# An earlier weight split and two later loads in a LayerNorm, attention and feed-forward kernel

## The chip, the cores and the metric

The kernel runs on one core of a Trainium2 chip. The metric is the device time of one execution in microseconds (us); lower is better. The core has five engines that each work through their own instructions in order: TensorE (PE: matrix products), VectorE (DVE), ScalarE (ACT), GpSimd (POOL) and SyncE (SP, which here only issues transfers). They wait for each other by semaphores. Transfers between memory and the on-chip buffers run on 16 DMA engines.

## The reference

```python
x  = A_x                                   # 2048 x 576
xn = layernorm(x)                          # (x - mean) / sqrt(var + 1e-5)
# A: local dilated attention, 32 heads of 18
q, k, v = split(xn @ wqkv)                 # wqkv: 576 x 1728
idx = pos[:, None] - 2 * arange(8)         # 8 positions, two apart; negative ones masked
attn = softmax(where(mask, q . k[idx] * 18 ** -0.5, -1e9))
A = (attn . v[idx]) @ wo
# B: feed-forward, 576 -> 4608 -> 576
h = relu(xn @ w1 + b1); h = h * h
B = h @ w2 + b2
out = x + A + B
```

Everything is float32.

## The kernel before

**Tiling.** The 2048 positions are four blocks (`b` = 0 to 3) of 512. The Q, K, V weights are four groups (`g` = 0 to 3, eight heads each). A "row" is one call of `qkv_row(b, g, j, i)`: 14 matmuls (L304) that give K, V and Q of 128 positions for one group; ScalarE copies the product out (L296) and issues its store to the scratch tensors `kvq` (L298), from which the attention later loads its rows.

**Split operands.** To keep float32 precision, each matmul operand is held as a high half (rounded by ScalarE) and a low half (the rest, subtracted by VectorE, L95). For the Q, K, V weights this is `split_wq(g, name)`: three high halves (`wq_hi`, L262) and three low halves (`wq_lo`, tiles `h`, `S` or `w1s` from the raw tiles `r`), handed out in three steps. Its last step may call a function, here the load of another group, because the raw tiles share four buffers: a new group can come only as low halves free them. A row of group g needs `split_wq(g)` to be done.

**Normalization.** Means and inverse deviations of block 1 are turned by TensorE, written to memory and read back spread over all partitions as tile `mb` (`load_mb`, L172). `normalize(b)` then subtracts and multiplies in place (tiles `w1r`, `w2r`), and makes the halves `X` and `x`: 8 steps. A row of block b needs it to be done.

**Order of the work.** The engines' order is the order of the program. Side work is written as generators: `run(pieces, k)` takes k steps from the list `pieces`, and when that is empty, from the attention queue (`side`). The attention of a block and group runs on VectorE in such steps; `offer(b, g)` queues it and its loads (`fetch`: tiles `q` and `kv`, on SP at first, later on GpSimd).

- `q0` does rows 0 to 25 before the first feed-forward pair: rows 0 to 3 are group 1 of block 0, 4 to 7 group 3, 8 to 11 group 2, and from row 12 on they are block 1. At r = 2 it issues `load_wq(2)` and `load_mb(1)`.
- `phase_a` runs the feed-forward of two blocks in 18 pairs of hidden tiles (`ffn_pair`, L524, L528, L493), `phase_b0` the second product of block 1 (tiles n = 0 to 35, 14 matmuls each, L493) together with the normalization and the rows of blocks 2 and 3. `load_w2(i)` brings the w2 tiles through three buffers, `load_h` the stored hidden tiles. `load_xt(3)` brings x of block 3 (L157, L160) into a buffer that block 0's output (`finish`, L757, L758) has to leave first.

Of the kernel before, what the change touches and what calls it, by code (L numbers as in the profile page):

```python
# [45 lines left out]
def block_kernel(ctx: ExitStack, tc: tile.TileContext, x, xt, wqkv, wo, w1, b1, w2, b2, out):  # L46
# [47 lines left out]
    def tt(out, a, b, op):  # L94
        return nc.vector.tensor_tensor(out=out, in0=a, in1=b, op=op)  # L95
# [14 lines left out]
    def open_x(b):  # L110
        X[b] = mt.tile([P, 2, NC - 1, TB], F32R, name=f"X{b % 2}")
        x4[b] = mt.tile([P, TB], F32R, name=f"x4{b % 2}")

    def four(dt=F32):
        return sb.tile([P, 2, TB], dt, name="r4", bufs=4)
# [39 lines left out]
    def load_xt(b):  # L155
        xm[b] = sb.tile([P, NC - 1, TB], F32, name="w1r", bufs=2)
        nc.sync.dma_start(xm[b], xt[b, :, :NC - 1])  # L157
        xf[b] = {1: lambda: sb.tile([P, DE], F32, name="w2r", bufs=3)[:, :TB],
                 2: lambda: sb.tile([P, TB], F32, name="xf"), 3: lambda: four()[:, 0]}[b]()
        nc.sync.dma_start(xf[b], xt[b, :, NC - 1])  # L160
# [13 lines left out]
    def normalize(b):  # L174
        open_x(b)
        for a in (0, 2):
            v = xm[b][:, a:a + 2]
            for k, op in enumerate((ALU.subtract, ALU.mult)):
                tt(v, v, mb[b][:, k:k + 1].to_broadcast([P, 2, TB]), op)
                if k:  # L180
                    nc.scalar.activation(X[b][:, 0, a:a + 2], v, AF.Copy)
                yield
        for k, op in enumerate((ALU.subtract, ALU.mult)):
            tt(xf[b], xf[b], mb[b][:, k], op)
        left_hi(x4[b], xf[b])
        yield
        for a in (0, 2):
            tt(X[b][:, 1, a:a + 2], xm[b][:, a:a + 2], X[b][:, 0, a:a + 2].bitcast(F32), ALU.subtract)
            yield
        left_lo(x4[b], xf[b])  # L190
        normed.add(b)
        yield

    def left_hi(to, v):
        nc.scalar.activation(to, v, AF.Copy)

    def left_lo(to, v):
        tt(to[64:], v[64:], to[64:].bitcast(F32), ALU.subtract)
# [49 lines left out]
    def load_wq(g, ks=range(3)):  # L248
        for k in ks:
            n = 2 if k < 2 else 1  # L250
            r = raws[g, k] = sb.tile([P, 2, QW], F32, name="r4", bufs=4)[:, :n]
            nc.sync.dma_start(r, wqkv[g, :, 2 * k:2 * k + n])
# [14 lines left out]
    def split_wq(g, name, then=lambda: None):  # L267
        open_wq(g, name)
        for k in range(4):
            if k < 3:  # L270
                wq_hi(g, k)
            if k:
                wq_lo(g, k - 1)
                if k == 3:
                    then()
                    split_up.add(g)
                yield
# [132 lines left out]
    def run(gens, k):  # L410

        while k > 0 and gens:
            try:
                next(gens[0])
                k -= 1
            except StopIteration:
                gens.pop(0)
        side(k)
# [355 lines left out]
    def phase_b0():  # L774
        b, r = 1, 0
        todo = [(2 + i, g, j) for g in range(G) for i in range(2) for j in range(NJ)]
        split_up.clear()
        open_stage()
        load_xt(3)
        load_wq(0)  # L780
        pieces = [normalize(2), once(load_mb, 3), split_wq(0, "S", lambda: load_wq(1)), normalize(3)]
        open_y(b)
        for n in range(NF):
            w2_hi()
            if n % 2 == 0:
                h_hi(0, n // 2 + 1)
            add(b, tile_products(b, n, hs[0, n // 2]))
            w2_lo()
            if n % 2 == 0:
                h_lo(0, n // 2 + 1)  # L790
            if n % 2 and n // 2 + 3 < NP:
                load_h(0, n // 2 + 3)
            run(pieces, 1 + n % 2 if n < 9 else 1)
            while r < 32 and 32 * (n - 6) > 22 * r:
                bb, g, j = todo[r]
                while bb not in normed or g not in split_up:
                    run(pieces, 1)
                qkv_row(bb, g, j, 2 + r % 3)
                r += 1
                if r == 2:  # L800
                    pieces.append(split_wq(1, "w1s", lambda: load_wq(2)))
                if r == 8:
                    pieces.append(split_wq(2, "S", lambda: load_wq(3)))
                if r == 16:
                    pieces.append(split_wq(3, "w1s"))
                if r == 24:
                    pieces.append(sums(1))
                if j == NJ - 1 and bb == 2:
                    offer(2, g)
                run(pieces, 2)  # L810
            if n == 20:
                load_w1(NP)
            if n == 25:
                assert not any(a != "x" and c < 2 for a, c, _ in loads)
                held[0] = True
            if n == 28:
                run_all(pieces)
                last_sum(1)
                complete(1)
                regroup(b, 0)  # L820
                regroup(b, 1)
                held[0] = False
                fetch()
                load_w1(NP + 1)
                for g in range(G):
                    offer(3, g)
            if n == 31:
                combine_w1(NP)
            if n == 33:
                residual(b)  # L830
            if n in (32, 33):
                c = 2 * (n - 32)
                o_hi(b, c), o_hi(b, c + 1)
                o_lo(b, c), o_lo(b, c + 1)
        o_hi(b, 4)
        o_lo(b, 4)
        open_left(b)
        load_left(b)
        for c in range(3):
            w2_hi()  # L840
            add(b, o_ops(b, c))
            w2_lo()
            if c == 1:
                w1_hi(NP, 0)
                w1_lo(NP, 0)

        def filler(i):
            if i < 2:
                add(b, o_ops(b, 3 + i), range(NC) if i else ())
            if i == 0:  # L850
                w1_hi(NP, 1)
                w1_lo(NP, 1)
            if i == 1:
                finish(b)

        return filler
# [247 lines left out]
    def q0():  # L1104
        todo = [(b, g, j) for b, g in ((0, 1), (0, 3), (0, 2), (1, 3), (1, 2), (1, 1), (1, 0)) for j in range(NJ)]
        pieces = [statistics(1), split_wq(3, "S")]

        waiting = []

        def row(r):  # L1110
            b, g, j = todo[r]
            while b and b not in normed or g not in split_up:
                run(pieces, 1)
            qkv_row(b, g, j, r % 5)
            if j == NJ - 1:
                def go(b=b, g=g):
                    offer(b, g)
                    if not b and g > 1:
                        offer({3: 2, 2: 3}[g])

                if r < 6:
                    waiting.append(go)
                else:
                    go()

        for r in range(len(todo) - 2):
            row(r)
            if r == 2:
                turn_mr(1, 7)
                run_all(pieces)  # L1130
                load_wq(2)
                load_mb(1)
                pieces += [normalize(1)]
            if r == 6:
                offer(0, 0)
                for late in waiting:
                    late()
                waiting.clear()
                lane[0] = nc.gpsimd
                pieces.insert(0, split_wq(2, "h", lambda: load_wq(0)))  # L1140
            if r == 10:
                load_w1(0)
            if r == 11:
                run_all(pieces)
            if r == 15:
                pieces.append(sums(0))
            if r == 19:
                split_up.discard(0)
                pieces.insert(0, split_wq(0, "h"))
            if r == 21:  # L1150
                run_all(pieces)
                for n in range(3):
                    load_w2(n)
                combine_w1(0)
                load_w1(1)
            if r in (24, 25):
                w1_hi(0, r - 24)
                w1_lo(0, r - 24)
            elif r != 3:
                run(pieces, 3 if r < 1 or 15 <= r < 20 else 1 if r > 20 else 2)  # L1160

        def filler(i):
            if i < 2:
                row(len(todo) - 2 + i)
            if i == 1:
                last_sum(0)

        return filler
# [68 lines left out]
```

## Time and profile before

| | |
|---|---|
| median of 3 runs | 1132.63 us (1131.63 to 1132.97) |
| profiled execution, its time | 1132.16 us |
| its span, first to last instruction | 1130.5 us |
| mean granted TensorE clock | 0.997 of full speed |
| DMA traffic | 216.50 MB, mean 192 GB/s |

A profile shows one execution. Timeline lines read: start and duration in us, engine, line of the kernel, operation, tiles out<-in, count, and in brackets how long the engine had stood idle and what ended that. "A <- B: total, times, longest" is a line of the list of waits. SPq lines are transfers being issued by SP, not their landing; a landing time counts from issue to the end of the transfer. Times are from the start of the span.

### The profile page before, as it was taken

How to read it: one execution, taken by the hardware profiler on the slowest of the kernel's cores; microseconds unless marked ns; L12 is line 12 of the kernel's file. 1: busy time of each engine (PE TensorE's matmuls, PEld its weight loads, DVE VectorE, ACT ScalarE, POOL GpSimd, SP SyncE). 2: the span in 40 equal slices, each digit the busy share in tenths (PEclk: the TensorE clock that was granted, in tenths of full speed). 3: DMA queues.
4: the chain of work that ended last, by engine and by line, in shares of the span. 5: the costliest groups of instructions: out<-in, count | busy, mean ns of one | idle time of the engine just before them, and what ended most of it. 6: DMA issues, size and time to landing. Idle time of an engine off the chain costs nothing.

```text
span 1130.5 us, 13846 instructions
## 1 busy us (share of the span) xinstructions
PE 1114.8 (99%) x5014; PEld 938.1 (83%) x5014; DVE 915.0 (81%) x1202; ACT 575.7 (51%) x801; POOL 118.1 (10%) x219
## 2 busy tenths in 40 slices
PE   9799999999999999999999999999999999999998
PEld 7699888888888888788889888888888888888887
DVE  7596888887978887779888979898989888786463
ACT  5334756566565654543333446656656566533341
POOL 4001001030200210001020101010202020101000
PEclk9899999999999999999999999999999999999999
DMA  8855546375583658865674855454545362568552
GB/s 291 294 197 168 162 140 205 121 151 202 170 218 101 214 195 284 285 222 182 226 270 131 316 167 174 161 180 137 191 146 197 129 210 95 179 210 300 180 170 89
DMA packets 88965, 216.50 MB, mean 192 GB/s; under 512 B 11960, under 2 KB 40384, under 8 KB 83520
## 3 DMA queue, kind: packets, MB, share of 16 engines
q1 hardware_dynamic: 52464, 148.95, 38.8%
q0 software_dynamic: 10544, 52.14, 14.5%
q10 hardware_dynamic: 25888, 14.53, 4.2%
q8 instruction: 39, 0.64, 0.2%
q14 instruction: 30, 0.25, 0.1%
HBM read 173.03 MB, written 42.55 MB: 191 GB/s over the span
## 4 chain that ended last, share of the span: by engine, by line
PE 90%; DVE 3%; DMA 2%; ACT 2%; issue 1%; POOL 0%; ACTq 0%; DVEq 0%; POOLq 0%; SPq 0%
PE p L493 42%; PE p L524 29%; PE p L304 13%; PE p L528 5%; DMA w2r<-in_w 1%; DVE w1s L95 1%; DMA mb<-mr 1%; PE p L1021 1%; DVE w2s L95 1%; DVE w1r L95 0%; ACT st L296 0%; POOL kvq L1173 0%; ACT h L535 0%; ACTq L298 0%; ACT w2s L466 0%
## 5 line engine op out<-in xcount | busy, mean ns | idle before, releaser
L493 PE MATMUL p<-h,w2s 128*128 128x512 f32 x2010 | 484.7, 390 | 2.2 <-ACT h L767 0.9
L493 PEld LDWEIGHTS p<-h,w2s 128*128 128x128 f32 x2010 | 376.8, 188 | 83.1 <-ACT h L767 1.3
L524 PE MATMUL p<-X,w1s 128*128 128x512 f32 x864 | 219.5, 389 | 0.2 <-DVE w1s L95 0.2
L524 PEld LDWEIGHTS p<-X,w1s 128*128 128x128 f32 x864 | 162.1, 188 | 34.1 <-DVE w1s L95 0.6
L95 DVE TENSOR_TENSOR w2s<-w2r,w2s 128x576 fp32r<-128x576 f32 x164 | 123.4, 754 | 65.5 <-ACT w2s L466 63.7
L466 ACT ACTIVATE w2s<-w2r 128x640 fp32r<-128x640 f32 x164 | 120.1, 734 | 109.9 <-PE p L493 91.3
L524 PE MATMUL p<-S,w1s 128*128 128x512 f32 x648 | 164.6, 389 | 0.0
L524 PEld LDWEIGHTS p<-S,w1s 128*128 128x128 f32 x648 | 121.5, 188 | 25.5 <-DVE r L95 0.3
L381 POOL DMA_DIRECT2D o<-q x128 | 69.4, 607 | 597.5 <-DVE q L95 595.7
L95 DVE TENSOR_TENSOR w1s<-w1r,w1s 128x1024 fp32r<-128x1024 f32 x72 | 88.1, 1224 | 33.6 <-ACT w1s L439 33.5
L531 ACT ACTIVATE r<-r,b1t 128x512 f32<-128x512 f32 x72 | 51.9, 721 | 107.6 <-DVE r L95 107.5
L296 ACT ACTIVATE st<-p 128x432 f32<-128x432 f32 x64 | 33.8, 529 | 117.0 <-PE p L304 107.4
L95 DVE TENSOR_TENSOR pr<-q,kv 128x1152 f32<-128x1152 f32 x64 | 86.8, 1356 | 1.6
L95 DVE TENSOR_TENSOR pr<-lg,kv 128x1152 f32<-128x1152 f32 x64 | 86.6, 1353 | 0.8
L353 DVE TENSOR_REDUCE lg<-pr 128x64 f32<-128x1152 f32 x64 | 86.4, 1349 | 0.8
L95 DVE TENSOR_TENSOR pr<-pr 128x576 f32<-128x576 f32 (+1 forms) x128 | 77.7, 607 | 3.8
L439 ACT ACTIVATE w1s<-w1r 128x1024 fp32r<-128x1024 f32 x72 | 75.7, 1052 | 5.1 <-PE p L493 4.2
L539 ACT ACTIVATE r<-r 128x1024 f32<-128x1024 f32 x72 | 75.4, 1051 | 0.1
L95 DVE TENSOR_TENSOR h<-r,h 128x1024 fp32r<-128x1024 f32 (+2 forms) x42 | 49.2, 1180 | 27.6 <-ACT r L539 23.8
L528 PE MATMUL p<-x,w1s 128*128 128x512 f32 x216 | 66.5, 389 | 0.0
L95 DVE TENSOR_TENSOR r<-p,r 128x512 f32<-128x512 f32 (+1 forms) x76 | 52.2, 687 | 13.0 <-ACT r L589 10.1
L304 PE MATMUL p<-w1s,X 128*128 128x432 f32 x288 | 60.3, 358 | 0.0
(138 smaller groups left out, 1115.5 us busy)
## 6 DMA issues: line engine op xcount, KB each, us to landing
w2r<-in_w SPq DMA_DIRECT2D x144, 320.0 KB, 3.1
kv<-kvq POOLq DMA_DIRECT2D x29, 1296.0 KB, 6.9
w1r<-in_w SPq DMA_DIRECT2D x36, 640.0 KB, 4.4
h<-r SPq DMA_DIRECT2D x36, 512.0 KB, 3.0
h<-h SPq DMA_DIRECT2D x36, 512.0 KB, 4.1
kvq<-st ACTq DMA_DIRECT2D x64, 216.0 KB, 2.9
r<-in_wqkv SPq DMA_DIRECT2D x16, 432.0 KB, 5.8
w2r<-in_wo SPq DMA_DIRECT2D x20, 320.0 KB, 3.0
```

Source lines behind the costliest of these rows:

```text
L95: return nc.vector.tensor_tensor(out=out, in0=a, in1=b, op=op)
L296: nc.scalar.activation(stage[0][:, j], p[:, :QW], AF.Copy)
L304: nc.tensor.matmul(p[:, :QW], l, r, start=k == 0, stop=k == len(mm) - 1)
L353: nc.vector.tensor_reduce(out=lg[:, j * HG:(j + 1) * HG].rearrange("p a w -> p w a"), in_=pr.rearrange("p w (a d) -> p w a d", d=DH), axis ...
L381: nc.gpsimd.dma_start(rows[:, i], q[i * L:(i + 1) * L, :, a:z])
L439: nc.scalar.activation(w1s[n, k][:, 0], raw1[n][:, 4 * k:4 * k + 4], AF.Copy)
L466: nc.scalar.activation(w2s[stream[i]][:, :DE], raw2[i], AF.Copy)
L493: nc.tensor.matmul(yp[b][c], v, a, start=c not in yb[b], stop=c in last and c not in [o[0] for o in ops[i + 1:]], skip_group_check=True)
L524: nc.tensor.matmul(to, l, r, start=start and i == 0, stop=i == len(mm) - 1, skip_group_check=True)
L528: nc.tensor.matmul(to, weight(LEFT, k, f), v, start=False, stop=k == 1, skip_group_check=True)
L531: nc.scalar.activation(to, a, AF.Relu, bias=b1t[:, f:f + 1])
L539: nc.scalar.activation(r, r, AF.Square)
```

## The change

Two edits. In `q0` the split of group 2 (whose last step calls `load_wq(0)`) is put into `pieces` at r = 4, in front of `normalize(1)`; before, `normalize(1)` was put there at r = 2 and the split was put ahead of what was left of it at r = 6. Since `load_wq(0)` is called from the split, its three transfers now stand ahead of the first attention loads (`offer(0, 0)` and the waiting offer, at r = 6) in SP's queue. In `phase_b0` the call `load_xt(3)` moves from the start to behind tile n = 3.

```diff
@@ phase_b0
         open_stage()
-        load_xt(3)
         load_wq(0)
         pieces = [normalize(2), once(load_mb, 3), split_wq(0, "S", lambda: load_wq(1)), normalize(3)]
...
                 run(pieces, 2)
+            if n == 3:
+                load_xt(3)
             if n == 20:
                 load_w1(NP)
@@ q0
                 run_all(pieces)
                 load_wq(2)
                 load_mb(1)
-                pieces += [normalize(1)]
+            if r == 4:
+                pieces += [split_wq(2, "h", lambda: load_wq(0)), normalize(1)]
             if r == 6:
                 offer(0, 0)
                 for late in waiting:
                     late()
                 waiting.clear()
                 lane[0] = nc.gpsimd
-                pieces.insert(0, split_wq(2, "h", lambda: load_wq(0)))
```

Instruction by instruction, the orders of TensorE and GpSimd stay as they were. On ScalarE and VectorE group 2's split now stands in front of the whole normalization of block 1, and two steps of the first attention come behind the sums of x (`sums(0)`) instead of ahead of them; from there the attention steps stand a little later among the first feed-forward pairs, until the orders agree again. On SP the three transfers of group 0 go ahead of the five first attention loads, and x of block 3 goes behind the h load of tile 3.

## The prediction

> **What bounds the kernel now.** I read the page first, then the list of waits of TensorE, then the timelines of the two places that this list names, engine by engine, then landing times and windows.
>
> ```profile
> span 1130.5 us, 13846 instructions
> ...
> PE 1114.8 (99%) x5014; PEld 938.1 (83%) x5014; DVE 915.0 (81%) x1202; ACT 575.7 (51%) x801; POOL 118.1 (10%) x219
> ...
> PE 90%; DVE 3%; DMA 2%; ACT 2%; issue 1%; POOL 0%; ACTq 0%; DVEq 0%; POOLq 0%; SPq 0%
> ```
> TensorE is busy for 99% of the span and carries 90% of the chain that ended last. So only time in which TensorE stands still, or runs slowly, can be won; other engines count only where TensorE waits for them. Its waits:
> ```profile
> PE p L304 <- ACT h L262: 6.8, 1, 6.8
> ...
> PE p L493 <- ACT h L767: 0.9, 1, 0.9
> PE p L493 <- ACT w2s L466: 0.8, 1, 0.8
> ```
> One wait stands out: a Q, K, V row (L304) for the high half of a weight group (L262). The two small ones (L767, L466) lie in phase_b0. The change touches exactly these two places.
>
> **Place one: group 2's split and block 1's normalization.** TensorE's timeline (start, duration):
> ```profile
> 40.72 2.50 PE L304 MATMUL p<-S,X 128*128 128x432 f32 x12
> ...
> 50.37 4.61 PE L304 MATMUL p<-h,X 128*128 128x432 f32 x12 [6.75 <-ACT h L262]
> ...
> 55.20 2.52 PE L304 MATMUL p<-h,X 128*128 128x432 f32 x12
> ```
> These are rows r = 7, 8 and 9 (each has 2 more matmuls behind these 12). A row takes 2.75 us at full speed: the chain has two rows in 5.49, in a line shown further down. Row 8, the first that reads group 2, could start at 40.72 + 2.75 = 43.47 and row 9 at 46.22. Row 9 started at 55.20: **8.98 us lost**, 6.75 idle and the rest a slow row 8 (4.61 for 2.51). The clock tells why; in this row of the windows view PEclk is the field before the last two:
> ```profile
> 50.00:55.00 5.00, 4.63 (x13) 3.82 (x14) 4.59 (x6) 2.00 (x4) 0.00 (x0) 0.57 1.00 369
> ```
> The granted clock was 0.57 right behind the gap, so without the gap the slow row goes too. The Trainium skill ("TensorE: Matmul & The Clock Gate", Part 1) says that an idle window of about 3.4 us halves the clock and a busy one restores it. By it, half speed for 3.4 us would cost 1.7 us, an estimate, and the loss would be 8.45 us, which would put the sum 0.5 us higher. The row measures 4.61 - 2.51 = 2.1 us and more in its end; I keep the 8.98.
>
> Why was group 2 late? VectorE, ScalarE and the load queue:
> ```profile
> 40.31 4.88 DVE L95 TENSOR_TENSOR w1r<-w1r,mb 128x1024 f32<-128x1024 f32 x4 [8.13 <-DMA mb<-mr]
> ...
> 50.35 2.54 DVE L95 TENSOR_TENSOR h<-r,h 128x864 fp32r<-128x864 f32 x3 [2.70 <-ACT h L262]
> 52.81 1.22 DVE L95 TENSOR_TENSOR X<-w1r,X 128x1024 fp32r<-128x1024 f32 x1
> 54.06 0.69 DVE L95 TENSOR_TENSOR x<-w2r,x 64x512 fp32r<-64x512 f32 x1
> 54.78 1.36 DVE L95 TENSOR_TENSOR pr<-q,kv 128x1152 f32<-128x1152 f32 x1
> ```
> ```profile
> 49.39 2.19 ACT L262 ACTIVATE h<-r 128x864 fp32r<-128x864 f32 x3 [0.49 <-ACT st L296]
> ```
> ```profile
> 31.55 1.31 SPq L252 DMA_DIRECT2D r<-in_wqkv  x3
> 33.38 0.33 SPq L172 DMA_DIRECT2D mb<-mr  x1
> ...
> 34.27 1.01 SPq L326 DMA_DIRECT2D kv<-kvq  x2
> ...
> 48.96 3.77 SPq L252 DMA_DIRECT2D r<-in_wqkv  x3
> ```
> Landing times, from the transfers of 29 to 45 us and from those of tile kv:
> ```profile
> r<-in_wqkv SPq DMA_DIRECT2D x2, 432.0 KB, 4.1
> ...
> r<-in_wqkv SPq DMA_DIRECT2D x1, 216.0 KB, 4.5
> ```
> ```profile
> DMA to landing us min/median/max: 6.6/9.9/12.3
> ```
> Group 2's raw weights were issued from 31.55 to 32.86, so they had landed by about 37.4. But their split stood behind the normalization, and that waited for mb until 40.31: VectorE stood idle for 8.13 us with the split's work at hand.
>
> **The change there.** No arithmetic is added or removed. I go through the new order.
>
> The split now stands behind row 4's output on ScalarE. Row 4 starts three rows before row 7, at 32.47, and ends at 35.22. From the first high half to the last low half the split took 50.35 + 2.54 - 49.39 = 3.50 us. Begun when row 4 ends, it would be done at 38.7; begun only when the last piece is in, at 40.9. I take 39.9, since the first piece lands near 35.7 (31.55 + 4.1) and row 4's output comes first. Row 8 needs it at 43.47: 3.6 us of cover, 2.6 at the late end. If this cover went, each microsecond beyond it would be TensorE's. **Gain 8.98 us.**
>
> The normalization comes behind it. mb had landed at 40.31; it now shares the queue with fewer bytes, so I take no later time for it. Before, VectorE did its part ahead of the split from 40.31 to 47.65 (50.35 less the 2.70 idle), 7.34 us, and its part behind from 52.81 to 54.75, 1.94 us. So it ends at 49.6 instead of 54.75. Row 12, the first of block 1, starts at 43.47 + 4 x 2.75 = 54.5: 4.9 us of cover.
>
> The queue: load_wq(0)'s three transfers move ahead of the first q and kv loads, and two of them wait for buffers that the split's first two low halves free, the second a little before the split's end. All five attention loads and load_w1(0) queue behind that. Near the split's end q goes, and the first K load near 40.3, 6 us later than before. Bounds for its landing from the tile's row: 46.9 (40.3 + 6.6) and 52.6 (40.3 + 12.3). The slowest before had a second kv load, mb and group 2 before it; I take 48, near the lower middle, because here only 648 KB of late group 0 pieces are ahead of q and K. VectorE wants K at 49.6. So it is free at 48, and 3.0 us late at worst. The Trainium skill ("DMA: Bandwidth & Descriptors", Queues, rings and completion order) speaks against this step: descriptors on an engine are consumed in ring order and a completion lands only behind that engine's earlier writes. By it alone K could not pass those transfers; the late K is a rival below, priced from rows. Nothing in this trace has K behind group 0's transfers.
>
> Does the earlier start survive to the feed-forward part?
> ```profile
> 70.49 1.25 DVE L95 TENSOR_TENSOR pr<-pr 128x576 f32<-128x576 f32 x2
> ...
> 73.40 1.22 DVE L95 TENSOR_TENSOR w1r<-w1r 128x1024 f32<-128x1024 f32 x1
> ...
> 101.34 1.23 DVE L95 TENSOR_TENSOR w1s<-w1r,w1s 128x1024 fp32r<-128x1024 f32 x1 [1.30 <-ACT w1s L439]
> ```
> ```profile
> 101.81 0.61 PE L524 MATMUL p<-X,w1s 128*128 128x512 f32 x2
> ```
> ```profile
> sum 320.00, PE 319.64 PEld 264.97 DVE 266.50 ACT 192.05 POOL 38.62; mean PE 18.80 PEld 15.59 DVE 15.68 ACT 11.30 POOL 2.27
> ```
> In the new order two steps of the first attention come behind the sums: 73.40 - 70.49 = 2.91 us less before them. The sums then start at 49.6 + (73.40 - 54.78) - 2.91 = 65.3, which is 8.1 us earlier. VectorE's work from there to the first w1 low half is the same. It was free at 100.04, 1.30 us before that step; now at 91.9. TensorE needs the step 8.98 us earlier, at 92.36. So 0.4 us are left, and K may land 0.4 us after 49.6. The two steps fall into the feed-forward pairs, where the windows from 100 to 420 us sum to PE 319.64 of 320 and DVE 266.50: VectorE has 53 us to spare. No cost.
>
> **Place two: x of block 3.**
> ```profile
> 443.27 15.25 PE L493 MATMUL p<-h,w2s 128*128 128x512 f32 x66 [0.16 <-DVE w1r L747]
> ...
> 463.63 6.64 PE L493 MATMUL p<-h,w2s 128*128 128x512 f32 x28 [0.89 <-ACT h L767]
> ```
> ```profile
> 450.64 7.75 DMA w2r<-in_w
> ...
> 470.27 5.49 PE p L304 x28
> 475.76 3.19 PE p L493 x14
> ```
> ```profile
> 445.94 0.51 SPq L758 DMA_DIRECT2D out<-r  x1
> 448.06 0.36 SPq L157 DMA_DIRECT2D w1r<-in_xt  x1
> ...
> 448.94 1.66 SPq L252 DMA_DIRECT2D r<-in_wqkv  x3
> 450.64 1.05 SPq L456 DMA_DIRECT2D w2r<-in_w  x2
> ```
> ```profile
> w2r<-in_w SPq DMA_DIRECT2D x144, 320.0 KB, 3.1
> ...
> w1r<-in_xt SPq DMA_DIRECT2D x6, 1024.0 KB, 6.9
> ```
> The queue stood at 446.45 until 448.06, when block 0's output had left x's buffer, then sent x and group 0, and only then w2 for tile 5. That w2 took 7.75 us, to 458.39, with its split still to come; TensorE waited 0.75 for it (the 0.8 of the waits), and the 0.89 behind it follows, since ScalarE and VectorE ran late after it. Without both, tile 5 starts at 458.52 and three tiles of 3.19 end at 468.09, against 470.27: **gain 2.18 us**. In the new order w2 is issued near 448.1 and lands between 451.2 (3.1) and 455.9 (7.75). Even then 2.6 us are left for its split before 458.52.
>
> ```profile
> 472.98 4.88 DVE L95 TENSOR_TENSOR w1r<-w1r,mb 128x1024 f32<-128x1024 f32 x4 [0.56 <-DMA mb<-mr]
> ```
> x now goes out behind the h load of tile 3, when that tile ends near 455.3, and lands near 462.2. Queued behind it: w2 for tiles 9 and 10, the next h load, mb of block 3. Tile 9 begins near 468.1 + 5.5 + 3.2 = 476.8, and x itself is wanted by VectorE's normalization near 472.98 - 2.18 = 470.8. About 14 and 8 us of cover: no cost.
>
> **Sum.** The profiled execution took 1132.16 us; minus 8.98 and 2.18 is 1121.0. The median of the runs is 0.47 higher, so 1121.4. In a measurement of this kernel 0.2% (2.3 us) is about what can be told from no change.
>
> **Rivals.**
> *Place two gives nothing* (w2 is held by something else, or x hurts where it now stands): for it, the earlier w2 waits from 432 on show the queue crowded there; against it, the cover above. 1121.4 + 2.2 = 1123.6. Chance 0.10.
> *The first K load is late*: for it, the row's maximum; against it, the bytes in flight. At 52.6, less the 0.4 us of slack, it costs 2.6 us: 1124.0. Chance 0.09.
> *The split does not come early* (weights land late, or ScalarE is held): for it, landing times vary; against it, 2.6 to 3.6 us of cover. Place one is lost in full only if the split still ends after mb's work: 1130.4. Chance 0.04.
> *Slower*: K gates all of VectorE's in-order work up to the feed-forward start, each microsecond beyond 50.0 costs one. It beats 11.2 us of gain and adds 0.2% only if K lands after 50.0 + 11.2 + 2.3 = 63.5, 23 us after its issue, nearly twice the longest row; then 1135 or more. Chance 0.03.
>
> **The numbers.** The forecast holds 0.74. The range goes from 1120.0 (the runs scatter by 0.7 either way, and some further hidden delay may go at place two) to 1124.3, which takes in the first two rivals. Faster by over 0.2%: 0.95; within: 0.02; slower: 0.03.
>
> **What would show it.** Right: the 6.75 us wait is gone, the granted clock stays at 1.0 from 40 to 60 us, row 9 starts near 46.2, the feed-forward part near 92.8, and the waits on L466 and L767 in phase_b0 are gone. Wrong: VectorE idle before its first attention step with a kv transfer as releaser, a longer wait of TensorE on w1s near 93, or a new wait in phase_b0 behind x's load.

## The result and the profile after

The changed kernel took **1124.77 us** (median of 6 runs, 1123.5 to 1125.66), the kernel before 1132.62 (6 runs, 1131.49 to 1133.38): a ratio of 0.9931, with a 95% interval of 0.9918 to 0.9944. It is faster by 7.9 us; the forecast was 11.2, and 1124.77 lies 0.5 us above the top of its range. The profiled execution took 1125.13 us. From its page:

```profile
span 1123.4 us, 13847 instructions
...
PE 1112.8 (99%) x5014; PEld 938.1 (84%) x5014; DVE 914.7 (81%) x1202; ACT 575.7 (51%) x801; POOL 117.7 (10%) x219
...
PE 87%; DVE 6%; DMA 3%; ACT 2%; issue 1%; SPq 0%; ACTq 0%; POOL 0%; DVEq 0%; POOLq 0%
```
TensorE's share of the chain that ended last fell from 90 to 87%, VectorE's rose from 3 to 6% and DMA's from 2 to 3%: somewhere the chain now runs through other engines instead of through matmuls. The list of TensorE's waits says where:
```profile
PE p L524 <- DVE w1s L95: 2.6, 1, 2.6
...
PE p L493 <- ACT h L767: 0.2, 1, 0.2
```
The 6.8 us on L262 are gone, and so are L466's 0.8 and most of L767's 0.9, as forecast. New is a wait of 2.6 us at the start of the feed-forward part (L524). TensorE's timeline at place one, rows 7, 8 and 9 (each line is the 12 long matmuls of a row), and the windows view there (the field before the last two is the granted clock):
```profile
42.21 2.50 PE L304 MATMUL p<-S,X 128*128 128x432 f32 x12
...
44.94 2.51 PE L304 MATMUL p<-h,X 128*128 128x432 f32 x12
...
47.68 2.52 PE L304 MATMUL p<-h,X 128*128 128x432 f32 x12
```
```profile
50.00:55.00 5.00, 5.00 (x28) 4.80 (x27) 2.79 (x3) 2.54 (x4) 0.00 (x0) 1.00 1.01 421
```
No gap, no slow row, and the clock is 1.00 where it was 0.57. To see where the rest of the time went, four points of TensorE's timeline are compared: the first row (r = 0), the first feed-forward matmul, the second group of these matmuls, and the first row of phase_b0. Before:
```profile
21.42 2.50 PE L304 MATMUL p<-w1s,X 128*128 128x432 f32 x12
...
102.62 1.19 PE L524 MATMUL p<-X,w1s 128*128 128x512 f32 x4 [0.19 <-DVE w1s L95]
...
470.11 2.51 PE L304 MATMUL p<-S,X 128*128 128x432 f32 x12
```
After:
```profile
22.90 2.52 PE L304 MATMUL p<-w1s,X 128*128 128x432 f32 x12
...
94.29 0.61 PE L524 MATMUL p<-X,w1s 128*128 128x512 f32 x2
97.48 1.19 PE L524 MATMUL p<-X,w1s 128*128 128x512 f32 x4 [2.57 <-DVE w1s L95]
98.74 1.53 PE L524 MATMUL p<-S,w1s 128*128 128x512 f32 x6
...
463.07 2.51 PE L304 MATMUL p<-S,X 128*128 128x432 f32 x12
```
(102.62 is the group behind the prediction's row at 101.81.)

| stretch | before, us | after, us | difference | forecast |
|---|---|---|---|---|
| start to r = 0 | 21.42 | 22.90 | +1.48 | 0 |
| r = 0 to the first L524 | 80.39 | 71.39 | **-9.00** | -8.98 |
| first L524 to its second group | 0.81 | 3.19 | **+2.38** | 0 |
| second group to the first row of phase_b0 | 367.49 | 365.59 | -1.90 | -2.18 |
| from there to the end of the span | 660.39 | 660.33 | -0.06 | 0 |

The sum is -7.10, which is the difference of the spans. Of the 4.1 us by which the profiles fall short of the forecast, 2.38 are the new wait, 1.48 a later start of the rows and 0.28 place two.

**Where the new wait begins** is 40 us earlier. VectorE (start, duration, and in brackets its idle time and releaser):
```profile
38.85 2.55 DVE L95 TENSOR_TENSOR h<-r,h 128x864 fp32r<-128x864 f32 x3 [5.18 <-ACT h L262]
41.71 4.88 DVE L95 TENSOR_TENSOR w1r<-w1r,mb 128x1024 f32<-128x1024 f32 x4 [0.32 <-DMA mb<-mr]
...
52.14 1.22 DVE L95 TENSOR_TENSOR X<-w1r,X 128x1024 fp32r<-128x1024 f32 x1 [3.09 <-ACT X L181]
...
54.12 1.36 DVE L95 TENSOR_TENSOR pr<-q,kv 128x1152 f32<-128x1152 f32 x1
```
The split is done at 41.4 and the normalization starts at once, but inside it VectorE stands for 3.09 us, because ScalarE has not made the second high half of X (L181). ScalarE (ACTq is a transfer that it issues):
```profile
44.23 1.06 ACT L181 ACTIVATE X<-w1r 128x1024 fp32r<-128x1024 f32 x1 [1.29 <-DVE w1r L95]
45.20 0.51 ACT L296 ACTIVATE st<-p 128x432 f32<-128x432 f32 x1
50.64 0.37 ACTq L298 DMA_DIRECT2D kvq<-st  x1
51.05 1.06 ACT L181 ACTIVATE X<-w1r 128x1024 fp32r<-128x1024 f32 x1 [5.34 <-DMA kv<-kvq]
```
Between X's two high halves, in program order, stand the output of row 7 (L296) and its store (L298). The output was copied at 45.7; the store went out at 50.64, and the bracket names a kv load as what ended ScalarE's 5.34 us. A store of row 7 uses no data of that load. The chain of waits gives the links with their times:
```profile
34.73 8.44 DMA kvq<-st
...
43.24 7.32 DMA kv<-kvq
...
50.64 0.37 ACTq L298
...
51.05 1.07 ACT X L181
```
In the built program the transfers of SP and ScalarE report their end on eight semaphores in rotation, and a transfer is issued only when the one before it on its semaphore has landed. The store of row 3 (34.73), the first K load (43.24) and the store of row 7 (50.64) have the same one; in the trace's records it is number 100 for all three, and each goes out just after the one before has landed (43.17, then 43.24; 50.56, then 50.64). So K was issued, though it reads other rows, 1.5 us after the queue had reached it (the q load ahead of it went out at 41.32 and took 0.38), when row 3's store landed; row 7's store had to wait for K; and X's second high half stood behind that store in ScalarE's order. Attention began at 54.12. The forecast's 49.6, moved by the 1.48 of the late start, is 51.08: 3.04 us later, and less the forecast's 0.4 us of slack that gives 2.6, against 2.38 measured at the feed-forward start.

### The profile page after: what moved, and what is told of

The parts are those of the page before. It is cut to its first block, busy times and chain, and to the rows that moved or that the text cites. A ratio compares the mean times of both kernels' runs of the same rounds, so it can differ in the third digit from the quotient of the medians.

```text
span 1123.4 us, 13847 instructions
## 1 busy us (share of the span) xinstructions
PE 1112.8 (99%) x5014; PEld 938.1 (84%) x5014; DVE 914.7 (81%) x1202; ACT 575.7 (51%) x801; POOL 117.7 (10%) x219
## 4 chain that ended last, share of the span: by engine, by line
PE 87%; DVE 6%; DMA 3%; ACT 2%; issue 1%; SPq 0%; ACTq 0%; POOL 0%; DVEq 0%; POOLq 0%
PE p L493 42%; PE p L524 29%; PE p L304 9%; PE p L528 5%; DVE pr L95 1%; PE p L1022 1%; DMA kvq<-st 1%; DVE w1s L95 1%; DMA kv<-kvq 1%; DMA w2r<-in_w 1%; DVE r L95 1%; DVE lg L353 0%; DVE w1r L95 0%; DVE w2s L95 0%; DMA r<-in_wqkv 0%
## 5 line engine op out<-in xcount | busy, mean ns | idle before, releaser
L524 PE MATMUL p<-X,w1s 128*128 128x512 f32 x864 | 219.5, 389 | 2.6 <-DVE w1s L95 2.6
L524 PEld LDWEIGHTS p<-X,w1s 128*128 128x128 f32 x864 | 162.1, 188 | 36.5 <-DVE w1s L95 3.0
L466 ACT ACTIVATE w2s<-w2r 128x640 fp32r<-128x640 f32 x164 | 120.1, 734 | 110.6 <-PE p L493 92.9
L524 PE MATMUL p<-S,w1s 128*128 128x512 f32 x648 | 164.6, 389 | 0.0
L524 PEld LDWEIGHTS p<-S,w1s 128*128 128x128 f32 x648 | 121.4, 188 | 25.5 <-DVE r L95 0.2
L296 ACT ACTIVATE st<-p 128x432 f32<-128x432 f32 x64 | 33.8, 528 | 104.5 <-PE p L304 89.7
```

The costliest lines, as they stand in the source:

```text
L296: nc.scalar.activation(stage[0][:, j], p[:, :QW], AF.Copy)
L466: nc.scalar.activation(w2s[stream[i]][:, :DE], raw2[i], AF.Copy)
L524: nc.tensor.matmul(to, l, r, start=start and i == 0, stop=i == len(mm) - 1, skip_group_check=True)
```

## The experiments

The first four ran on one chip, the next three on another, the last two on the first again, each group beside runs of the kernel before (1132.09, 1132.57 and 1132.32 us). In the texts on record theory A is the one above: a store on ScalarE that cannot go out until the K load has landed costs the 2.4 us at the feed-forward start. Its rivals put the missing time at place two (B), at a K load or queue that is late for VectorE itself (C), or into attention steps that were moved and are paid for later (D).

**Edit 1 alone** (before, with the split moved to r = 4 and x of block 3 left where it was).

```diff
     # q0
-                pieces += [normalize(1)]
+            if r == 4:
+                pieces += [split_wq(2, "h", lambda: load_wq(0)), normalize(1)]
...
-                pieces.insert(0, split_wq(2, "h", lambda: load_wq(0)))
```


> Edit one alone (group 2's split first), x of block 3 left where it was. Theory A (a store of ScalarE that waits for the first K load gives part of place one back): place one is worth 8.98 less 2.4, and place two is missing, 1.8 by the two profiles: 1126.6 us, with TensorE's 2.6 us wait on w1s still there. Theory B (place two gave nothing, as the first rival said): 1124.8, as with both edits.

Measured: 1128.3 us (1126.94 to 1131.65), ratio 0.9969, interval 0.9957 to 0.9981. TensorE's timeline at the feed-forward start:
```profile
96.63 1.19 PE L524 MATMUL p<-X,w1s 128*128 128x512 f32 x4 [3.00 <-DVE w1s L95]
```
The new wait is here too, without the second edit: it belongs to the split. By this profile (1127.09 us) the span from r = 0 (21.60) to 96.63 is 75.03 us, where before has 81.20: 6.17 of the 8.98 are left. Behind 96.63 this profile is 0.89 us longer than before, with 1.3 us of waits on L466 instead of 0.8. The median of the runs is only 3.8 below before: 1.7 us above theory A's 1126.6, and further still from B's 1124.8. The four runs with a mean granted clock of 1.000 took 1126.94 to 1128.42, so the clock does not explain it all; the rest stays open.

**Edit 2 alone** (before, with only `load_xt(3)` moved).

```diff
     # phase_b0
-        load_xt(3)
...
+            if n == 3:
+                load_xt(3)
```


> Edit two alone (x of block 3 behind tile 3). Theory A and the profiles: the two waits on L466 and L767 go, 1.8 us less than before: 1130.8 us. The prediction's own term: 2.18 less, 1130.4. The first rival: no change, 1132.6.

Measured: 1130.71 us (1129.25 to 1131.28), ratio 0.9985, interval 0.9976 to 0.9993. TensorE:
```profile
102.35 1.20 PE L524 MATMUL p<-X,w1s 128*128 128x512 f32 x4 [0.17 <-DVE w1s L95]
...
461.23 6.66 PE L493 MATMUL p<-h,w2s 128*128 128x512 f32 x28 [0.16 <-ACT h L767]
467.72 2.51 PE L304 MATMUL p<-S,X 128*128 128x432 f32 x12
```
From 102.35 to 467.72 are 365.37 us, where before took 367.49: 2.12 less, against 2.18 forecast. The rival "place two gives nothing" falls. In runs the gain is 1.4 (0.8 to 2.7 by the interval). The two edits taken singly give 3.8 + 1.4 = 5.2 us, and both together 6.5 to 7.9 in three measurements. Of the difference, 0.9 us by the profiles is what edit 1 alone loses behind the feed-forward start; the rest is open.

**X's high halves ahead of row 7's store** (changed kernel; four steps at r = 6 and none at r = 7, so that ScalarE makes the rest of the high halves before row 7's output; nothing is added or left out).

```diff
-                run(pieces, 3 if r < 1 or 15 <= r < 20 else 1 if r > 20 else 2)
+                run(pieces, 3 if r < 1 or 15 <= r < 20 else 1 if r > 20 else 4 if r == 6 else 0 if r == 7 else 2)
```


> The changed kernel with block 1's normalization steps 4 and 5 in front of row 7, so that ScalarE makes X's second high half and x4's before it comes to the store of row 7; VectorE's and SP's orders and every transfer stay. Theory A (the store, which waits for the first K load, held ScalarE for 5 us and with it X's high half): VectorE's 3.1 us of idle in the normalization goes, the w1s wait falls from 2.6 to about 0.2 us, 2.4 us less: 1122.4 us. Theory C (the first K load or the queue itself is late, so VectorE would wait anyway) and theory D (the two attention steps moved behind the sums cost it): no change, 1124.8.

Measured: 1122.53 us (1121.73 to 1122.6), ratio 0.9915, interval 0.9902 to 0.9927. ScalarE, VectorE and TensorE:
```profile
49.48 0.37 ACTq L298 DMA_DIRECT2D kvq<-st  x1
```
```profile
46.67 2.35 DVE L95 TENSOR_TENSOR X<-w1r,X 128x1024 fp32r<-128x1024 f32 x2
...
49.77 1.36 DVE L95 TENSOR_TENSOR pr<-q,kv 128x1152 f32<-128x1152 f32 x1
...
64.33 0.42 DVE L363 TENSOR_REDUCE sm<-lg 128x32 f32<-128x256 f32 x1 [2.09 <-ACT lg L361]
```
```profile
94.74 1.19 PE L524 MATMUL p<-X,w1s 128*128 128x512 f32 x4 [0.75 <-DVE w1s L95]
```
Row 7's store is as late as before, but nothing that VectorE wants stands behind it. X's two low halves follow each other, attention begins at 49.77, and the wait at the feed-forward start falls from 2.57 to 0.75. This shows the cause: only the order on ScalarE changed; the instructions of the other engines stand in the same order. From r = 0 (21.96) to the second group the profile has 72.78 us, where the changed kernel has 74.58: 1.80 less. The 2.2 us between the medians are not all from this, since this profile's r = 0 also came 0.94 earlier. Theory A had expected a wait of 0.2; what is left comes from 64.33, where VectorE has waited 2.09 us for an attention step on ScalarE behind other late stores (0.56 in the kernel before).

**The attention loads ahead of group 0's** (changed kernel; the queue order of the kernel before, with the split still early).

```diff
-                pieces += [split_wq(2, "h", lambda: load_wq(0)), normalize(1)]
+                pieces += [split_wq(2, "h"), normalize(1)]
...
                 lane[0] = nc.gpsimd
+                load_wq(0)
```


> The changed kernel, but group 0's raw weights are loaded behind the five first attention loads, as before the change; the split stays early. K then lands some 4 to 6 us sooner. Theory C (K's landing sets it): the wait on w1s is gone, 1122.4 us. Theory A: by the built program the stores of rows 5, 6 and 7 then share completion semaphores with the first q load, the third kv load and a weight load, so the store of row 6, ahead of both high halves of X, waits for the third kv load (near 50 us): the normalization is late again, 1124.8 to 1127 us.

Measured: 1131.0 us (1129.74 to 1132.42), ratio 0.9991, interval 0.9982 to 0.9999. ScalarE, then TensorE:
```profile
52.73 0.37 ACTq L298 DMA_DIRECT2D kvq<-st  x1
53.14 1.06 ACT L181 ACTIVATE X<-w1r 128x1024 fp32r<-128x1024 f32 x1 [11.05 <-DMA kv<-kvq]
```
```profile
101.49 2.07 PE L524 MATMUL p<-X,w1s 128*128 128x512 f32 x4 [4.30 <-DVE w1s L95]
```
Of SyncE's queue:
```profile
34.73 1.06 SPq L326 DMA_DIRECT2D kv<-kvq  x2
...
42.37 0.39 SPq L326 DMA_DIRECT2D kv<-kvq  x1
```
The first two kv loads go out at 34.73 instead of 43.24, and it is worse. Fewer bytes ahead of K should have helped if K's landing for VectorE were the trouble; K landed at 44.31, and theory C falls. Theory A has the reason: in the built program the store of row 6 shares a semaphore with the third kv load (42.37, landed at 52.65) and stands in front of both high halves of X; the one at 53.14 is the first. ScalarE stood 11.05 us instead of 5.34. The direction was expected, the price (1124.8 to 1127 us) was underrated: TensorE waited 1.19 and 4.30 us at the feed-forward start, and the granted clock was 0.84 and then 0.50 there (95 to 100 and 100 to 105 us).

**The changed kernel again** (no edit).

> The changed kernel once more, nothing edited, for its start: in its first profile the first row of the Q, K, V part (r = 0) began at 22.90 us, 1.48 later than in the profile before. If that is scatter from run to run, this profile shows r = 0 between 21.4 and 22.9, as the other runs' (21.60 to 21.96), and 1124.8 us in the median; if the change itself delays the start, 22.9 again.

Measured: 1126.11 us (1124.38 to 1128.77), ratio 0.9943, interval 0.9931 to 0.9956. Its profiled execution was the slowest of these runs, 1128.77. TensorE and the windows view:
```profile
98.42 2.07 PE L524 MATMUL p<-X,w1s 128*128 128x512 f32 x4 [3.49 <-DVE w1s L95]
...
100.72 2.76 PE L524 MATMUL p<-S,w1s 128*128 128x512 f32 x6
```
```profile
95.00:100.00 5.00, 1.58 (x4) 1.29 (x5) 4.90 (x7) 1.10 (x2) 0.00 (x0) 0.72 0.16 48
100.00:105.00 5.00, 5.00 (x17) 4.11 (x16) 0.95 (x3) 0.58 (x1) 0.00 (x0) 0.60 0.38 131
```
The same wait was 3.49 us here and the clock fell behind it; the two groups of matmuls took 2.07 and 2.76 us, for 1.19 and 1.53 in the first profile, 2.1 us more. The wait itself is not its whole price: the slower clock behind it comes on top. The start, for which this was run, was late again: r = 0 began at 22.92.

**Two attention steps fewer ahead of the feed-forward** (X's high halves first, and no step at r = 14 either).

```diff
-                ... else 4 if r == 6 else 0 if r == 7 else 2)
+                ... else 4 if r == 6 else 0 if r in (7, 14) else 2)
```


> The kernel with the halves first, and two further attention steps (the end of the softmax and one product, 2.6 us of VectorE) behind the sums: no step at r = 14. Theory A: what is left of the w1s wait there, 0.75 us, comes from VectorE being 2.1 us late behind an exponential that stands on ScalarE behind held-up stores; with 2.6 us less ahead of the feed-forward part the wait goes to about 0.2: 1122.0 us. Theory D (attention steps moved later are paid for in the feed-forward pairs): 1122.5 or more, with waits of TensorE there.

Measured: 1123.86 us (1123.24 to 1126.06), ratio 0.9928, interval 0.9915 to 0.9942. TensorE:
```profile
94.15 1.20 PE L524 MATMUL p<-X,w1s 128*128 128x512 f32 x4 [0.17 <-DVE w1s L95]
...
634.75 3.51 PE L493 MATMUL p<-h,w2s 128*128 128x512 f32 x14 [0.88 <-ACT w2s L466]
...
639.31 9.86 PE L493 MATMUL p<-w1s,w2s 128*128 128x512 f32 x42 [1.05 <-ACT w2s L466]
```
The wait at the start is down to 0.17, but two new ones of 0.88 and 1.05 stand 540 us later in the profile. This fits theory D, by which a step left for later is paid for elsewhere, but does not show it. The attention steps stand in another order all the way to these waits, and ahead of the first of them ScalarE had waited 3.47 us for an h tile (1.53 in the kernel with the high halves first). A wait of this size also comes without an edit: the second profile of that kernel has one of 1.30 us (on L747, at 436.11), the first has not. The version is no better than the one without this step.

**The gap filled** (before, with 26 bf16 matmuls on constant data ahead of row 8; extra work into an unused result).

```diff
+            if r == 7:
+                idle = bank(7)
+                for _ in range(26):
+                    nc.tensor.matmul(idle, warm[:, :P], warm, start=True, stop=True)
```


> The kernel before, with 26 matmuls on constant data (about 5.7 us, results unused) between row 7 and row 8, so that TensorE is busy in the 6.75 us gap; nothing else changes and the gap stays as long. If the slow row 8 (4.61 us for 2.51) is the price of the clock that fell in the gap, row 8 takes 2.5 us up to its own wait for low halves, the granted clock stays at 1.0, and the time falls by 1.0 to 2.1 us: 1130.0 to 1131.1. If row 8 is slow because it waits for the low halves piece by piece, it stays slow: 1132.1.

Measured: 1131.68 us (1131.13 to 1134.18), ratio 0.9996, interval 0.9987 to 1.0004. TensorE and the windows view:
```profile
43.92 5.56 PE L1144 MATMUL p<-lg 128*128 128x512 bf16 x25
50.97 0.67 PE L304 MATMUL p<-h,X 128*128 128x432 f32 x2 [1.49 <-ACT h L262]
52.06 3.78 PE L304 MATMUL p<-h,X 128*128 128x432 f32 x10 [0.43 <-DVE h L95]
```
```profile
50.00:55.00 5.00, 3.60 (x10) 3.03 (x11) 4.02 (x5) 2.60 (x4) 0.00 (x0) 0.72 0.98 344
```
This was to tell how much of the slow row 8 is the clock's. It is inconclusive: the clock fell to 0.72 all the same, after 1.49 us of idle time.

**The changed kernel a third time, and X's high halves first a second time**, side by side (no new edit).

> The changed kernel a third time, side by side with the next one. Theory A: a wait on w1s of 2.5 to 3.5 us, 1124.5 to 1126.5 us. Its first row (r = 0), at 22.9 us in both profiles so far: 21.4 to 22.0 if that was chance, 22.9 if it belongs to this kernel.

> The kernel with the halves first once more, on the same chip as the changed kernel: theory A gives a wait on w1s under 1 us and 2 to 3 us less than the changed kernel, 1122 to 1123 us. If the first result came from another chip or chance, the two agree.

Measured: 1125.35 us (1123.71 to 1127.66), ratio 0.9935 (0.9921 to 0.9948), and 1122.11 us (1121.57 to 1123.67), ratio 0.991 (0.9896 to 0.9924). The second kernel's row:
```profile
94.39 1.20 PE L524 MATMUL p<-X,w1s 128*128 128x512 f32 x4 [0.75 <-DVE w1s L95]
```
Its wait is 0.75 again, where the changed kernel's was 3.37 (with a granted clock of 0.81 from 95 to 100 us). The changed kernel's r = 0 began at 23.20, this one's at 21.62. The version with X's high halves first is the best of all that ran: 3.2 us below the changed kernel here (part of it the start), 2.2 in the first measurement of each, and some 10 below the kernel before.

## Why the prediction was right or wrong

*Place one, the gain of 8.98: right.* From r = 0 to the first feed-forward matmul the time fell by 9.00. Moved by the late start, the split's end at 39.9 becomes 41.38; it was 41.40. Row 9 at 46.22 becomes 47.70; it was 47.68. The prediction's lower figure of 8.45 was 0.5 short. That the slow row 8 would go with the gap was right as well. The filled gap did not settle how much of it was the clock's, but the clock records in the trace of before do: half speed from 47.50 to 54.33 us, which covers the first 3.96 us of the row that began at 50.37 and so accounts for 1.98 of its 2.10 us.

*The queue and the normalization, "so it is free at 48": this step failed.* K landed at 50.56 (43.24 + 7.32), inside the bounds (46.9 to 52.6, moved by 1.48) and half a microsecond before VectorE would have taken it, at 51.03 (54.12 - 3.09). So the transfer that was asked about was in time. But the step counted VectorE's own time alone (7.34 and 1.94 us) and knew one waiter for K, VectorE's first attention step. The other was row 7's store on ScalarE, and with it everything queued behind that store, X's second high half first. The normalization therefore ended 3.04 us later than forecast, and that went through to the feed-forward start, as the step "K may land 0.4 us after 49.6" had said of any lateness there: +2.38. The rival "the first K load is late" had nearly the price (2.6) with the wrong mechanism. It had a chance of 0.09, because the chance was asked of the bytes in flight only; and the range ended just above its 1124.0, as if it would come alone, while this wait came with 1.48 us at the start and 0.28 at place two. The prediction's mark for being wrong, "a longer wait of TensorE on w1s near 93", is what came.

*mb "no later": right*, it made VectorE wait 0.32 us. *Two attention steps moved, no cost: right for this change* (the last stretch of the table differs by 0.06), but two more brought nothing in the one kernel that tried it.

*Place two, 2.18: right in kind, a little large.* The second edit alone gave 2.12 by its profile, and the changed kernel 1.90. The waits on L466 and L767 went from 0.8 and 0.9 to none and 0.2, and no wait of TensorE came behind x's load.

*The start, 1.48 us later: not foreseen.* The instructions up to r = 0 are the same in both kernels. In all three profiles of the changed kernel r = 0 starts at 22.90 to 23.20; in the other eight at 21.42 to 21.96, and three of these are of kernels that are the same as the changed one up to row 6. A group of seven first matmuls, before and then after, shows how slowly TensorE ran there:
```profile
7.96 1.82 PE L1021 MATMUL p<-h,X 128*128 128x432 f32 x7
```
```profile
9.17 2.57 PE L1022 MATMUL p<-h,X 128*128 128x432 f32 x7
```
The windows view from 5 to 15 us, of the changed kernel's second profile and of the kernel with X's high halves first:
```profile
5.00:15.00 10.00, 8.45 (x38) 6.74 (x37) 7.96 (x24) 4.98 (x12) 5.76 (x10) 0.83 1.04 399
```
```profile
5.00:15.00 10.00, 8.84 (x46) 6.39 (x45) 8.73 (x25) 5.12 (x14) 5.92 (x10) 1.00 1.05 395
```
The changed kernel got 38 matmuls done in these 10 us instead of 46, at a clock of 0.83; in its third profile the clock is 0.83 again. In the first the view says 1.00, but there the trace's clock records begin only at 11.2 us (at 5.0 to 7.8 in the other ten), and its matmuls are as slow, so half speed up to 11.2 is likely. So the late start goes with a slow TensorE clock in two profiles, and probably in the first. Why the clock was low there in this kernel alone, and whether three of three is chance, stays open. Without the late start and without the new wait, the profile would have met the forecast within 0.3 us.

## What to carry to other kernels

When a load is moved to a later place, ask not only who reads its data but which later transfers, on any engine, wait for its completion, and what compute is queued behind those on the issuing engine. Where an engine both computes and issues stores, put the compute that others wait for ahead of a store that may stall: here that order alone made the stretch up to the feed-forward part 1.8 us shorter (more where the clock had fallen behind the wait), and no transfer was moved for it. A shortened critical stretch also eats the slack behind it, so a forecast that leaves 0.4 us should price what comes due next, and add that price to the other risks instead of taking the worst one.

## What the runs showed of the hardware

A transfer that has to wait holds up the engine that issues it, arithmetic included: ScalarE stood 5.34 and 11.05 us behind a store that could not go out, for most of that time with the next activation's input made (in the first case at 46.6, when VectorE's four steps on w1r ended; the activation began at 51.05). The Trainium skill ("DMA: Bandwidth & Descriptors", Anatomy of one DMA — SWDGE (gpsimd) path) says that a transfer's semaphore wait happens on the issuing sequencer before dispatch; the traces agree. That two unrelated transfers are tied by a shared completion semaphore comes from the built program and from the semaphore numbers in the traces.

The granted clock behind TensorE's idle time at the feed-forward start stayed at 1.00 after 2.57 and 3.00 us, and fell to 0.81 after 3.37 and to 0.72 and then 0.60 after 3.49. Counted from the end of the wait, the next Q, K, V row began 1.4 us later behind the wait of 3.37, and 2.2 us later behind the 3.49, than in the first profile. This fits the scatter of the changed kernel: its five runs with a mean clock of 1.000 took 1123.5 to 1125.13 us, the twelve with less 1124.47 to 1128.77 (halves-first: 1121.57 to 1123.67). The Trainium skill ("TensorE: Matmul & The Clock Gate", Part 1) gives an idle window of about 3.4 us for this; these four waits agree with it, the filled gap, where the clock fell after 1.49 us of idle time, does not if the window is read as one wait.

The clock records allow a reading that takes in the filled gap. In every trace here the clock changes at whole multiples of 3.41 us from its first change (in the changed kernel's third profile at 98.13 and 101.55 us, for example). In the stretch of 3.41 us ahead of a fall in mid-kernel TensorE was busy for at most 0.44 of the time: 0.44 in the filled gap, 0.34 and 0.14 in the changed kernel's second and third profiles. With 0.50 (edit 1 alone) and 0.52 (the changed kernel's first profile) the clock stayed up. So it may be the busy share of such a stretch that counts, not the length of one wait. No run tests this, and at the start of the kernel it fails: there the clock fell behind a share of 0.67 (the changed kernel's third profile) and stayed up behind one of 0.66 (X's high halves first).
